# The dense part's products read their moving operand in turns from two runs of 256 words

## The chip, the cores and the metric

The kernel runs on one core of a Trainium2 chip. The metric is the device time of one execution in microseconds (us). A core has a matrix engine (TensorE, PE in the profile, with its weight loads as PEld), VectorE (DVE), ScalarE (ACT), GpSimd (POOL), and a queue engine (SyncE, SP) that issues transfers here. A product on TensorE holds a stationary operand of up to 128 columns and streams a moving operand of up to 512 columns through it; the result goes to PSUM.

## The reference

Three stages: attention with two fixed masks, a mixture of experts with soft slots, and a dense two-layer network. The change lies in the last one, and its inputs are:

```python
def _moe_ref(x, phi, w1, w2):          # 2304 tokens, 512 wide; 8 experts with 4 slots each
    logits = x @ phi
    ...                                # slot_out: 32 rows of 512, one for each slot
    c = softmax(logits, axis=1)        # 2304 x 32
    return c @ slot_out

def _moe2_ref(x, w_in, w_out):         # w_in 512 x 2048, w_out 2048 x 512
    h = x @ w_in
    g = np.where(h > 0.0, h, np.exp(np.minimum(h, 0.0)) - 1.0)
    return g @ w_out                   # 2304 x 512
```

The weights w_in and w_out come as 64-bit floats and are decoded to 32 bits on the chip.

## The kernel before

Attention and experts take the first 126 us. After them the kernel never forms the experts' output x. Since x = c @ slot_out, the hidden layer is h = c @ (slot_out @ w_in), and the kernel forms M = slot_out @ w_in (tile `M4`, 2048 columns) in two-part numbers that fill 128 rows.

The moving operand of the hidden layer is `cT`: the routing weights c, transposed, one column for each of the 2304 tokens. It is copied from `c4` by `emit_ct` (line 1026), sixteen copies of 32x576 elements: for each of four batches four row groups, in turn on ScalarE, GpSimd and, for two of them, VectorE. These copies are written between the last experts' products.

The dense part is a list of units. A unit (`unit_nodes`, line 1256) is one block of 128 hidden columns (f, 16 of them) for one group of tokens (`groups`: four groups of 512 tokens and one of 256). It consists of:

- one product at line 1264, stationary 128 columns of `M4`, moving 512 (or 256) columns of `cT`;
- exponential and ReLU on ScalarE (lines 1268, 1271), the combination on VectorE (line 1274), which together give g;
- the split of g in a high part on ScalarE (line 1280, f_hi) and a low part on VectorE (line 1284, f_lo). [...]
- for each of the 4 (or 2) token tiles of 128 three products with w_out at lines 1312 to 1314: high by high, high by low, low by high. Here the moving operand is a row block of w_out, 512 columns, itself split in two parts (lines 1213 and 1216).

The very last token tile of the last unit has its three products in two halves of 256 columns. [...] Units are counted from 0. All products of the dense part, 79 units of them and unit 0, accumulate in PSUM, six banks for the outputs and two for the hidden layer. An output tile whose run of f blocks ends is evicted to `part` (lines 1347, 1349) or, at last, added up in `ob` and stored (lines 1353 and 1360).

Beside that the weights are decoded, four steps a block: line 991 on ScalarE, lines 995, 999 and 1005 on VectorE. Lines 991 and 999 read every second 32-bit word of the 64-bit numbers. M's further columns are formed at lines 1153 to 1180.

The order of all this work on the engines is set by `list_order` (line 87), a list scheduler that runs when the program is built. It gets nodes with an engine, an estimated duration, what they depend on and a key (when they are due), and takes them by key. The due times step on by the estimated product times: `now += groups[gi][1] / 512 * ((3.6 if u < FULL else 2.72) + 0.2267)` (line 1121), where 2.72 is four token tiles of 0.68, and 0.68 and 0.2267 are also the durations of the nodes of lines 1317 and 1292. Before the dense part has filled up, warm-up products (line 1373, bfloat16, 256 columns) fill waits of TensorE. Loads on SyncE's queue stand in the same list.

Of the kernel before, what the change touches and what calls it, by code (L numbers as in the profile page):

```python
# [9 lines left out]
F32R = mybir.dt.float32r  # L10
I32 = mybir.dt.int32
BF16 = mybir.dt.bfloat16
AF = mybir.ActivationFunctionType
# [6 lines left out]
def attn_moe_mlp(ctx, tc, q, k, v_l, v_s, phi, w1, w2, w_in, w_out, out):  # L20
    nc = tc.nc
    B, S, D = 4, q.shape[2] // 4, 64
    NT, DM = out.shape
# [46 lines left out]
    FULL = 1  # L70
    FT, FW, M0 = 7.5, 0.9, ((0, 128), (128, 128), (256, 256))
# [184 lines left out]
    with tc.manual_schedule():  # L256
# [765 lines left out]
        cT = pers[:, 0:NT].rearrange("p (b s) -> p b s", b=B).bitcast(F32R)  # L1022
        M4 = pers[:, NT:NT + DFF].bitcast(F32R)
        e0r = e0.bitcast(F32R)

        def emit_ct(eng, a, b):
            o, i = cT[32 * a:32 * a + 32, b], c4[32 * b:32 * b + 32, a // 2].bitcast(F32R)
            if eng == "A":
                nc.scalar.activation(out=o, in_=i, func=AF.Copy)
            else:  # L1030
                (nc.vector if eng == "V" else nc.gpsimd).tensor_copy(out=o, in_=i)
# [54 lines left out]
        cTf = cT.rearrange("p b s -> p (b s)")  # L1086
        NF = DFF // 128
        groups = [(t, min(512, NT - t)) for t in range(0, NT, 512)]
# [167 lines left out]
        def unit_nodes(u):  # L1256
# [35 lines left out]
            x = link("h", node("P", 0.2267 * z, [m_done[f]], T - 4.1 - SL, f_h, ("h", rel_h)))  # L1292
# [9 lines left out]
            for s in range(n // 128):  # L1302
                def f_o(s=s):
                    if f == f0:
                        ops[si, gi, s] = ps_out.tile([128, DM], F32, tag="o", name="ops")
                    o, c = ops[si, gi, s], slice(128 * s, 128 * s + 128)
                    if full:
                        nc.tensor.matmul(o, t["g"][:, c], dec_of["o", f // 4, f % 4], start=(f == f0), stop=False)
                        return
                    hi, lo = w_tile(wo_hi, 0, f).bitcast(F32R), w_tile(wo_lo, 5, f).bitcast(F32R)  # L1310
                    for x in halves(u, s):
                        nc.tensor.matmul(o[:, x], t["hi"][:, c], hi[:, x], start=(f == f0), stop=False)  # L1312
                        nc.tensor.matmul(o[:, x], t["hi"][:, c], lo[:, x], start=False, stop=False)  # L1313
                        nc.tensor.matmul(o[:, x], t["lo"][:, c], hi[:, x], start=False, stop=(f == f1 - 1 and x.stop == 512))  # L1314

                rel_o = []
                y = link("o", node("P", 0.9 if full else 0.68, [x, d3[1, f // 4, f % 4, 0] if full else w_done[f]],
                                   T + 0.68 * s, f_o, ("o", rel_o) if f == f0 else None))
# [6 lines left out]
                if f == f0:  # L1325
                    o_rel.append(rel_o)
                    o_due.append(T + 0.68 * s)
                    part_n[si, gi, s] = len(o_rel) - 1
                if f == f1 - 1:
                    ev_n.append((si, gi, s, f0, f1, y, T + 0.68 * s, halves(u, s)))  # L1330
# [51 lines left out]
def _lay(np, q, k, v, moe_phi, **rest):  # L1382
# [17 lines left out]
    return dict(rest, q=lay(q), k=lay(k), v_l=vl, v_s=vs, moe_phi=phi, moe_w1=w1, moe_w2=w2)  # L1400
# [25 lines left out]
```

## Time and profile before

| | us |
|---|---|
| median of 3 timed runs | 358.36 (358.03 to 359.21) |
| the profiled execution, its time | 357.83 |
| its span, first to last instruction | 356.1 |
| TensorE busy | 336.8 |
| VectorE busy | 260.8 |
| ScalarE busy | 248.7 |
| GpSimd busy | 57.4 |

Times in the profile count from the first instruction of the span. [...] Each execution has a time outside the span (1.7 us in the profiled one).

### The profile page before, as it was taken

To read this page: it belongs to the slowest core of one execution; us is meant where nothing else is said; L and a number is where in the kernel's file an instruction comes from. 1 tells how busy PE (TensorE), PEld (TensorE's weight loads), DVE (VectorE), ACT (ScalarE), POOL (GpSimd) and SP (SyncE) were. 2 spreads that over 40 slices of the span, in tenths; PEclk is the share of its full clock that TensorE was granted. 3 is DMA by queue.
4 is the path that set the end of the run, shared out by engine and by line. 5 is a ranking of instruction groups with operands and counts; after the bars stand their busy time and mean duration, and the time that the engine had idled before them with its cause. 6 is when DMAs were issued, how large, how long until landed. Compare 5 with 4: busy or idle time off the path is not lost.

```text
span 356.1 us, 6955 instructions
## 1 busy us (share of the span) xinstructions
PE 336.8 (95%) x2678; PEld 249.6 (70%) x2678; DVE 260.8 (73%) x574; ACT 248.7 (70%) x488; POOL 57.4 (16%) x106
## 2 busy tenths in 40 slices
PE   5589899998999999999999999999999999999995
PEld 4378777773333257787888788888878888888884
DVE  6999889743706069999999999997755674576741
ACT  9588999982216079999977877767656666666650
POOL 8888534520214000000000000000000000000000
PEclk9999999999999999999999999999999999999999
DMA  7999999999999998750006041000000030032301
GB/s 280 401 418 411 424 421 421 424 407 420 430 424 417 404 403 323 250 221 0 3 0 238 0 162 74 2 0 0 2 0 1 2 119 0 31 118 88 118 2 59
DMA packets 15328, 70.50 MB, mean 198 GB/s; under 512 B 1600, under 2 KB 2112, under 8 KB 12352
## 3 DMA queue, kind: packets, MB, share of 16 engines
q1 hardware_dynamic: 15296, 70.06, 49.3%
q8 instruction: 21, 0.34, 0.4%
q14 instruction: 11, 0.09, 0.1%
HBM read 65.34 MB, written 4.72 MB: 197 GB/s over the span
## 4 chain that ended last, share of the span: by engine, by line
PE 74%; DVE 8%; DMA 6%; ACT 4%; POOL 4%; issue 2%; DVEq 0%; SPq 0%; POOLq 0%
PE ops L1312 18%; PE ops L1314 18%; PE ops L1313 18%; DMA q<-in_moe_w_dram 6%; PE hps L1264 5%; PE s_ps L923 3%; ACT bd L657 2%; DVE sc L589 2%; PE o_ps L670 2%; PE mps L1153 1%; ACT xw L696 1%; PE xtps L786 1%; DVE sm L613 1%; POOL bd L659 1%; DVE ss L604 1%
## 5 line engine op out<-in xcount | busy, mean ns | idle before, releaser
L1274 DVE SCALAR_TENSOR_TENSOR g<-hps,g 128x512 f32<-128x512 f32 (+1 forms) x80 | 50.7, 634 | 17.8 <-ACT g L1271 17.3
L1268 ACT ACTIVATE g<-hps 128x512 f32<-128x512 f32 (+1 forms) x80 | 44.8, 560 | 13.6 <-PE hps L1264 12.2
L1271 ACT ACTIVATE g<-g 128x512 f32<-128x512 f32 (+1 forms) x80 | 47.5, 594 | 1.5
L1280 ACT ACTIVATE ghi<-g 128x512 fp32r<-128x512 f32 (+1 forms) x40 | 23.7, 591 | 18.3 <-DVE g L1274 16.5
L1314 PE MATMUL ops<-w,glo 128*128 128x512 f32 (+1 forms) x93 | 36.0, 387 | 0.0
L1280 ACT ACTIVATE rings<-g 128x512 fp32r<-128x512 f32 (+1 forms) x39 | 23.6, 606 | 17.3 <-DVE g L1274 16.5
L1312 PE MATMUL ops<-wh,rings 128*128 128x512 f32 x80 | 31.6, 396 | 0.0
L1312 PE MATMUL ops<-w,ghi 128*128 128x512 f32 (+1 forms) x81 | 31.4, 388 | 0.0
L1313 PE MATMUL ops<-w,ghi 128*128 128x512 f32 (+1 forms) x81 | 31.4, 387 | 0.0
L1313 PE MATMUL ops<-wl,rings 128*128 128x512 f32 x80 | 31.2, 390 | 0.0
L1314 PE MATMUL ops<-wh,glo 128*128 128x512 f32 x80 | 31.2, 390 | 0.0
L1264 PE MATMUL hps<-pers 128*128 128x512 f32 (+1 forms) x80 | 30.3, 380 | 0.0
L657 ACT ACTIVATE bd<-tr 32x288 f32<-32x288 f32 (+1 forms) x60 | 28.7, 479 | 1.3
L1313 PE MATMUL ops<-w,rings 128*128 128x512 f32 x64 | 25.0, 391 | 0.0
L1312 PE MATMUL ops<-w,rings 128*128 128x512 f32 x64 | 25.0, 391 | 0.0
L1314 PE MATMUL ops<-wh,rings 128*128 128x512 f32 x62 | 24.3, 392 | 0.0
L1312 PE MATMUL ops<-wh,ghi 128*128 128x512 f32 x62 | 24.2, 391 | 0.0
L1313 PE MATMUL ops<-wl,ghi 128*128 128x512 f32 x62 | 24.2, 391 | 0.0
L1314 PE MATMUL ops<-w,rings 128*128 128x512 f32 x52 | 20.2, 389 | 0.0
L1284 DVE TENSOR_TENSOR glo<-g,ghi 128x512 fp32r<-128x512 f32 (+1 forms) x24 | 15.2, 633 | 6.8 <-ACT ghi L1280 4.5
L1314 PEld LDWEIGHTS ops<-w,glo 128*128 128x128 f32 x93 | 17.5, 188 | 3.6
L670 PE MATMUL o_ps<-bd,v 128*64 128x128 f32 x288 | 18.1, 276 | 1.2 <-ACT bd L657 0.9
(230 smaller groups left out, 757.8 us busy)
## 6 DMA issues: line engine op xcount, KB each, us to landing
v<-in_moe_w_dram SPq DMA_DIRECT2D x3, 2048.0 KB, 11.8
w<-in_moe_w_in_dram SPq DMA_DIRECT2D x3, 2048.0 KB, 8.0
out_dram<-ob SPq DMA_DIRECT2D x17, 256.0 KB, 2.0
w<-in_moe_w_dram SPq DMA_DIRECT2D x2, 2048.0 KB, 11.6
xw<-in_moe_w_dram SPq DMA_DIRECT2D x4, 1024.0 KB, 11.9
xw<-in_moe_w_out_dram SPq DMA_DIRECT2D x2, 2048.0 KB, 7.8
q<-in_q_dram SPq DMA_DIRECT2D x6, 576.0 KB, 8.0
kB<-in_k_dram SPq DMA_DIRECT2D x8, 288.0 KB, 7.5
```

The lines of the kernel that those rows point to most:

```text
L657: nc.scalar.activation(out=o, in_=i, func=AF.Copy)
L670: nc.tensor.matmul(o[64 * e:64 * e + 64, j, :], v_t[p][:, max(i - 1 + k, 0), e, :], pt[:, 4 * j + 2 * e + k], start=(k == 0), stop=(k == 1),)
L923: nc.tensor.matmul(hp[32 * g:32 * g + 32, :], siT[:, POS[c], :], w_at(2 * a + g // 2, 0, 2 * c + g % 2), start=(c == CO[0]), stop=(c == CO ...
L1264: nc.tensor.matmul(t["ps"], M4[:, 128 * f:128 * f + 128], cTf[:, t0:t0 + n], start=True, stop=True)
L1268: nc.scalar.activation(out=t["g"], in_=t["ps"], func=AF.Exp)
L1271: nc.scalar.activation(out=t["g"], in_=t["g"], func=AF.Relu, scale=-1.0, bias=1.0)
L1274: nc.vector.scalar_tensor_tensor(out=t["g"], in0=t["ps"], scalar=0.0, in1=t["g"], op0=ALU.max, op1=ALU.subtract)
L1280: nc.scalar.activation(out=t["hi"], in_=t["g"], func=AF.Copy)
L1284: nc.vector.tensor_tensor(out=t["lo"], in0=t["g"], in1=t["hi"].bitcast(F32), op=ALU.subtract)
L1312: nc.tensor.matmul(o[:, x], t["hi"][:, c], hi[:, x], start=(f == f0), stop=False)
L1313: nc.tensor.matmul(o[:, x], t["hi"][:, c], lo[:, x], start=False, stop=False)
L1314: nc.tensor.matmul(o[:, x], t["lo"][:, c], hi[:, x], start=False, stop=(f == f1 - 1 and x.stop == 512))
```

## The change

The products at lines 1264, 1308 and 1312 to 1314 get another access pattern for the moving operand, and for the output a pattern that is the same dense run in other words. `turns` takes a run of n words as two halves and reads them alternately: word 0 of the first, word 0 of the second, word 1 of the first, and so on. For the results to stand where they stood, the operand must be stored with its even elements in the first half and its odd elements in the second. For `cT` the copies do this, in pieces that end at the groups' bounds; for w_out the host does it with the columns. The stationary operands are as they were. The planner's numbers for a product go from 0.2267 to 0.216, and for a token tile from 0.68 to 0.648.

```diff
+    PO, PH = 0.648, 0.216
...
-        cT = pers[:, 0:NT].rearrange("p (b s) -> p b s", b=B).bitcast(F32R)
+        cTf = pers[:, 0:NT].bitcast(F32R)
...
+        def turns(v):
+            return v.rearrange("p (a x) -> p x a", a=2)
+
+        def pairs(v):
+            return v.rearrange("p (x a) -> p x a", a=2)
+
         def emit_ct(eng, a, b):
-            o, i = cT[32 * a:32 * a + 32, b], c4[32 * b:32 * b + 32, a // 2].bitcast(F32R)
...
+            for t0, n in groups:
+                u0, u1 = max(t0, S * b), min(t0 + n, S * b + S)
+                if u0 >= u1:
+                    continue
+                o = turns(cTf[32 * a:32 * a + 32, t0:t0 + n])[:, (u0 - t0) // 2:(u1 - t0) // 2]
+                i = pairs(c4[32 * b:32 * b + 32, a // 2, u0 - S * b:u1 - S * b].bitcast(F32R))
...
-            now += groups[gi][1] / 512 * ((3.6 if u < FULL else 2.72) + 0.2267)
+            now += groups[gi][1] / 512 * ((3.6 if u < FULL else 4 * PO) + PH)
...
-                nc.tensor.matmul(t["ps"], M4[:, 128 * f:128 * f + 128], cTf[:, t0:t0 + n], start=True, stop=True)
+                nc.tensor.matmul(
+                    pairs(t["ps"]), M4[:, 128 * f:128 * f + 128], turns(cTf[:, t0:t0 + n]), start=True, stop=True
+                )
...
-                        nc.tensor.matmul(o, t["g"][:, c], dec_of["o", f // 4, f % 4], start=(f == f0), stop=False)
+                        nc.tensor.matmul(
+                            pairs(o), t["g"][:, c], turns(dec_of["o", f // 4, f % 4]), start=(f == f0), stop=False
+                        )
...
-                    hi, lo = w_tile(wo_hi, 0, f).bitcast(F32R), w_tile(wo_lo, 5, f).bitcast(F32R)
+                    hi, lo = turns(w_tile(wo_hi, 0, f).bitcast(F32R)), turns(w_tile(wo_lo, 5, f).bitcast(F32R))
                     for x in halves(u, s):
-                        nc.tensor.matmul(o[:, x], t["hi"][:, c], hi[:, x], start=(f == f0), stop=False)
...
+                        y, q = pairs(o[:, x]), slice(x.start // 2, x.stop // 2)
+                        nc.tensor.matmul(y, t["hi"][:, c], hi[:, q], start=(f == f0), stop=False)
...
+    wo = rest["moe2_w_out"]
+    wo = wo.reshape(wo.shape[0], -1, 2).transpose(0, 2, 1).reshape(wo.shape)
```

The copies, on VectorE, stand between the last decoding ahead of the dense part and the transposition that forms the slots' matrix (`pers` holds `cT`, c is `c4`, xw the decoded weights). Before:

```order
L999 SCALAR_TENSOR_TENSOR xw<-kA,xw 128x256
L1005 SCALAR_TENSOR_TENSOR xw<-kA,xw 128x256
L1031 COPY pers<-c_1492 32x576 x2
L1076 STREAM_TRANSPOSE soT<-s_ps_96 128x128
L995 TENSOR_SCALAR xw<-xw 128x512
```

And after, where lines are those of the changed kernel:

```order
L1000 SCALAR_TENSOR_TENSOR xw<-kA,xw 128x256
L1006 SCALAR_TENSOR_TENSOR xw<-kA,xw 128x256
L1045 COPY pers<-c_1492 32x224x2
L1045 COPY pers<-c_1492 32x64x2
L1045 COPY pers<-c_1492 32x160x2
L1045 COPY pers<-c_1492 32x128x2
L1090 STREAM_TRANSPOSE soT<-s_ps_96 128x128
```

Two copies have become four, with pairs of words as their innermost step; on GpSimd eight have become sixteen and on ScalarE six twelve, at the same places.

In the dense part nearly the same products follow each other on TensorE. What the planner's new numbers move lies mostly on VectorE and ScalarE. One place is VectorE from the low part of unit 7 to that of unit 8 (the rows that write glo or rings are low parts, L1274 is the combination, L995, L999 and L1005 are decoding steps, wl is the low part of w_out). Before:

```order
L1284 TENSOR_TENSOR glo_1797<-g,ghi_1796 128x512
L1005 SCALAR_TENSOR_TENSOR xw<-xw 128x512
L995 TENSOR_SCALAR xw<-xw 128x512
L1274 SCALAR_TENSOR_TENSOR g<-hps,g 128x512
L999 SCALAR_TENSOR_TENSOR xw<-w_0_1_1743,xw 128x512
L995 TENSOR_SCALAR xw<-xw 128x512
L1284 TENSOR_TENSOR glo_1798<-g,rings 128x512
```

And after (1298 is the low part, 1288 the combination, 996, 1000 and 1006 the decoding, 1228 w_out's low part, 1192 a piece of M):

```order
L1298 TENSOR_TENSOR glo_1813<-g,ghi_1812 128x512
L1192 SCALAR_TENSOR_TENSOR pers<-mp,negm,mps 128x256
L996 TENSOR_SCALAR xw<-xw 128x512
L1006 SCALAR_TENSOR_TENSOR xw<-xw 128x512
L1000 SCALAR_TENSOR_TENSOR xw<-w_0_1_1759,xw 128x512
L1228 TENSOR_TENSOR wl_1809<-xw,wh_1808 128x512
L1006 SCALAR_TENSOR_TENSOR xw<-w_0_1_1759,xw 128x512
L996 TENSOR_SCALAR xw<-xw 128x512
L1288 SCALAR_TENSOR_TENSOR g<-hps,g 128x512
L1000 SCALAR_TENSOR_TENSOR xw<-w_0_1_1759,xw 128x512
L1228 TENSOR_TENSOR wl_1809<-xw,wh_1808 128x512
L1298 TENSOR_TENSOR glo_1814<-g,rings 128x512
```

Ten rows stand between the two low parts where five stood; the piece of M and the low parts of w_out came later or earlier by one unit.

## Rows read from the trace of the kernel before

**Rows 1.** The page's head: span, busy time of each engine; chain of work.

```profile
span 356.1 us, 6955 instructions
...
PE 336.8 (95%) x2678; PEld 249.6 (70%) x2678; DVE 260.8 (73%) x574; ACT 248.7 (70%) x488; POOL 57.4 (16%) x106
...
PE 74%; DVE 8%; DMA 6%; ACT 4%; POOL 4%; issue 2%; DVEq 0%; SPq 0%; POOLq 0%
PE ops L1312 18%; PE ops L1314 18%; PE ops L1313 18%; DMA q<-in_moe_w_dram 6%; PE hps L1264 5%; PE s_ps L923 3%; ACT bd L657 2%; DVE sc L589 2%; PE o_ps L670 2%; PE mps L1153 1%; ACT xw L696 1%; PE xtps L786 1%; DVE sm L613 1%; POOL bd L659 1%; DVE ss L604 1%
```

**Rows 2.** Stretches: bounds and length, busy us of engines, granted clock, DMA share, GB/s.

```profile
150.00:160.00 10.00, 10.00 (x46) 8.29 (x45) 9.88 (x18) 10.00 (x20) 0.00 (x0) 1.00 0.61 212
170.00:180.00 10.00, 10.00 (x45) 8.26 (x44) 10.00 (x18) 9.66 (x19) 0.00 (x0) 1.00 0.00 1
220.00:230.00 10.00, 10.00 (x45) 8.28 (x45) 10.00 (x19) 7.24 (x13) 0.00 (x0) 1.00 0.01 2
260.00:270.00 10.00, 10.00 (x45) 8.24 (x44) 5.41 (x8) 6.00 (x11) 0.00 (x0) 1.00 0.00 0
```

**Rows 3.** By line: ns min/median/max, first and last start; from the timeline: start, us.

```profile
L1264 PEld LDWEIGHTS hps<-pers x16: 187/188/188, 276.2 to 320.4; 128*128 128x128 f32 x16
L1264 PE MATMUL hps<-pers x16: 389/390/390, 276.4 to 320.6; 128*128 128x512 f32 x16
...
L1264 PEld LDWEIGHTS hps<-pers x6: 187/188/189, 336.0 to 342.8; 128*128 128x128 f32 x6
L1264 PE MATMUL hps<-pers x6: 277/278/278, 336.2 to 343.1; 128*128 128x256 f32 x6
...
L1308 PE MATMUL ops<-xw,g x4: 592/593/593, 131.9 to 133.2; 128*128 128x512 f32 x4
...
L1373 PE MATMUL wps<-ident x23: 272/273/283, 128.1 to 134.0; 128*128 128x256 bf16 x23
...
130.29 1.48 PE L1373 MATMUL wps<-ident 128*128 128x256 bf16 x12
...
131.93 1.88 PE L1308 MATMUL ops<-xw,g 128*128 128x512 f32 x4
```

**Rows 4.** The chain before the dense part (start, us, what) and TensorE's last product.

```profile
101.41 22.16 DMA q<-in_moe_w_dram
...
351.94 0.28 PE L1314 MATMUL ops<-w,glo 128*128 128x256 f32 x1
```

**Rows 5.** Timeline of the copies on three engines: start, us, idle time ahead.

```profile
105.37 5.59 POOL L1031 CAST pers<-c 32x576 fp32r<-32x576 f32 x8 [14.01 <-issue]
...
109.82 4.13 ACT L1029 ACTIVATE pers<-c 32x576 fp32r<-32x576 f32 x6
126.06 0.38 ACT L1065 ACTIVATE y<-o_ps 128x256 f32<-128x256 f32 x1 [12.11 <-PE o_ps L1012]
...
115.11 0.92 DVE L1031 CAST pers<-c 32x576 fp32r<-32x576 f32 x2
```

**Rows 6.** Timeline: low parts of units 8 and 14, and their first products.

```profile
152.11 0.69 DVE L1284 TENSOR_TENSOR glo<-g,rings 128x512 fp32r<-128x512 f32 x1
...
155.60 0.39 PE L1312 MATMUL ops<-wh,rings 128*128 128x512 f32 x1
...
173.24 0.68 DVE L1284 TENSOR_TENSOR glo<-g,ghi 128x512 fp32r<-128x512 f32 x1
...
175.02 0.39 PE L1312 MATMUL ops<-wh,ghi 128*128 128x512 f32 x1
```

**Rows 7.** Groups by line, 150 to 250 us: count, busy us, mean ns, idle ahead.

```profile
L1271 ACT ACTIVATE g<-g 128x512 f32<-128x512 f32 x34 | 22.0, 647 | 0.5
...
L991 ACT ACTIVATE xw<-w 128x512 f32<-128x512 f32 x15 | 10.4, 725 | 0.0
...
L991 ACT ACTIVATE xw<-xw 128x512 f32<-128x512 f32 x8 | 5.0, 685 | 1.4 <-DMA xw<-in_moe_w_out_dram 1.4
...
L999 DVE SCALAR_TENSOR_TENSOR xw<-w,xw 128x512 int32<-128x512 int32 x16 | 10.9, 684 | 0.0
```

More of the change, by code (lines that the diff above doesn't have):

```diff
@@ L1021, in attn_moe_mlp @@
         ND = dec.shape[1]
-        cT = pers[:, 0:NT].rearrange("p (b s) -> p b s", b=B).bitcast(F32R)
+        cTf = pers[:, 0:NT].bitcast(F32R)
         M4 = pers[:, NT:NT + DFF].bitcast(F32R)
         e0r = e0.bitcast(F32R)
-        def emit_ct(eng, a, b):
-            o, i = cT[32 * a:32 * a + 32, b], c4[32 * b:32 * b + 32, a // 2].bitcast(F32R)
[L1028 to L1031, printed above, removed]
+        groups = [(t, min(512, NT - t)) for t in range(0, NT, 512)]
+        def turns(v):
+            return v.rearrange("p (a x) -> p x a", a=2)
+        def pairs(v):
+            return v.rearrange("p (x a) -> p x a", a=2)
+        def emit_ct(eng, a, b):
+            for t0, n in groups:
[4 more added lines that the diff above has]
+                i = pairs(c4[32 * b:32 * b + 32, a // 2, u0 - S * b:u1 - S * b].bitcast(F32R))
+                if eng == "A":
+                    nc.scalar.activation(out=o, in_=i, func=AF.Copy)
+                else:
+                    (nc.vector if eng == "V" else nc.gpsimd).tensor_copy(out=o, in_=i)
         for e in range(NE - 1):
@@ L1084, in attn_moe_mlp @@
         ps_out = ctx.enter_context(tc.tile_pool(name="ps_out", bufs=6, space=PSUM))
-        cTf = cT.rearrange("p b s -> p (b s)")
         NF = DFF // 128
-        groups = [(t, min(512, NT - t)) for t in range(0, NT, 512)]
         dec_of = {("w", 0, c): dec[:, c] for c in range(4)}
@@ L1290, in link @@
                 return x
-            x = link("h", node("P", 0.2267 * z, [m_done[f]], T - 4.1 - SL, f_h, ("h", rel_h)))
+            x = link("h", node("P", PH * z, [m_done[f]], T - 4.1 - SL, f_h, ("h", rel_h)))
             x = link("e", node("A", 0.05 + 0.43 * z, [x], T - 3.7 - SL, f_e, ("g", rel_g)))
@@ L1307, in f_o @@
                     if full:
-                        nc.tensor.matmul(o, t["g"][:, c], dec_of["o", f // 4, f % 4], start=(f == f0), stop=False)
+                        nc.tensor.matmul(
+                            pairs(o), t["g"][:, c], turns(dec_of["o", f // 4, f % 4]), start=(f == f0), stop=False
+                        )
                         return
-                    hi, lo = w_tile(wo_hi, 0, f).bitcast(F32R), w_tile(wo_lo, 5, f).bitcast(F32R)
+                    hi, lo = turns(w_tile(wo_hi, 0, f).bitcast(F32R)), turns(w_tile(wo_lo, 5, f).bitcast(F32R))
                     for x in halves(u, s):
-                        nc.tensor.matmul(o[:, x], t["hi"][:, c], hi[:, x], start=(f == f0), stop=False)
-                        nc.tensor.matmul(o[:, x], t["hi"][:, c], lo[:, x], start=False, stop=False)
-                        nc.tensor.matmul(o[:, x], t["lo"][:, c], hi[:, x], start=False, stop=(f == f1 - 1 and x.stop == 512))
+                        y, q = pairs(o[:, x]), slice(x.start // 2, x.stop // 2)
+                        nc.tensor.matmul(y, t["hi"][:, c], hi[:, q], start=(f == f0), stop=False)
+                        nc.tensor.matmul(y, t["hi"][:, c], lo[:, q], start=False, stop=False)
+                        nc.tensor.matmul(y, t["lo"][:, c], hi[:, q], start=False, stop=(f == f1 - 1 and x.stop == 512))
                 rel_o = []
-                y = link("o", node("P", 0.9 if full else 0.68, [x, d3[1, f // 4, f % 4, 0] if full else w_done[f]],
-                                   T + 0.68 * s, f_o, ("o", rel_o) if f == f0 else None))
+                y = link("o", node("P", 0.9 if full else PO, [x, d3[1, f // 4, f % 4, 0] if full else w_done[f]],
+                                   T + PO * s, f_o, ("o", rel_o) if f == f0 else None))
                 if full:
@@ L1326, in unit_nodes @@
                     o_rel.append(rel_o)
-                    o_due.append(T + 0.68 * s)
+                    o_due.append(T + PO * s)
                     part_n[si, gi, s] = len(o_rel) - 1
                 if f == f1 - 1:
-                    ev_n.append((si, gi, s, f0, f1, y, T + 0.68 * s, halves(u, s)))
+                    ev_n.append((si, gi, s, f0, f1, y, T + PO * s, halves(u, s)))
         for u in range(len(work)):
```

2 lines of the change are left out of this document (1 added, 1 removed).

## The prediction

> **What bounds the kernel now.** I read the page's head and its chain of work first [rows 1]. TensorE is busy for 336.8 of 356.1 us, and of the chain that ended last 54% are the three products of lines 1312 to 1314 and 5% the product of line 1264. That is the dense part, from 134 us to 352 us. [...] A TensorE record overlaps the next one (0.39 us long, but started every 0.23 us), so a busy share of 1 is not yet a proof; the pitch is. In the steady stretch sixteen line-1264 products start between 276.4 and 320.6 us [rows 3], one for each unit of work, and a unit is thirteen products of 512 columns (one of line 1264, four times three). 44.2 us / 15 / 13 = 226.7 ns from start to start, with no gap anywhere in it. TensorE's own rate bounds 218 us of the 356.
>
> What sets 226.7 ns? [...] The weight load is not the bound: a 256-column product of the dense part has the same 188 ns load record as a 512-column one, and its length is smaller by 112 ns [rows 3], as the columns are halved.
>
> **The change part by part.** *The moving reads.* [...] No row shows the interleaved read itself, so I bound its pitch. [...] Above: the reads of every second word that other engines do here [rows 7]. ScalarE's line 991 reads with a step of two words and takes 685 to 725 ns where line 1271, which reads a dense row, takes 647 ns, 6% to 12% more. VectorE's line 999 takes 684 ns with such a read and line 1284 takes 0.68 to 0.69 us without [rows 6], no difference. 6% on top of 226.7 ns would be 240 ns.
>
> How many: 16 blocks of the hidden layer by 18 token tiles less the 2 tiles of the float32 unit are 286 groups of three. One of them is split in halves of 256. Line 1264 has 64 products of 512 and 16 of 256 columns. That makes 855 + 64 = 919 products of 512 columns, each 226.7 - 215.7 = 11.0 ns shorter: 10.1 us. The 22 of 256 columns give 5 ns each (278 against 273): 0.1 us. Sum of the gain on TensorE: **10.2 us**. [...]
>
> *The start* of the dense part does not move: it waits for the last expert weights, which land at 123.6 us after a transfer of 22 us on the chain [rows 4]. *The end* keeps its tail: from the last product at 351.94 us, eviction and stores to 356.1 us [rows 4].
>
> *The copies into the moving operand.* Sixteen copies of 32x576 become thirty-two shorter ones (POOL 8 to 16, ScalarE 6 to 12, VectorE 2 to 4), with a destination in two runs. Before, one takes 0.66 us on POOL, 0.68 on ScalarE, 0.45 on VectorE [rows 5]. If the second piece costs as much as a whole copy did, and it cannot well cost more than that, POOL ends 5.6 us later, at 116.6 us, ScalarE 4.1 us later, at 118.1 us, VectorE 0.9 us later, at 116.9 us. Each engine has nothing else until 126 us (ScalarE idles 12.1 us there), and the first reader is the product at 129.8 us. Cost on the path: nothing. Were that cover gone, it would be ScalarE's 4.1 us.
>
> *The host's order of w_out's columns* and the outputs: the products write PSUM in the old order, so evictions and stores are the same instructions. Decoding w_out reads the same bytes. Nothing.
>
> *The faster TensorE and what feeds it.* Each unit needs two VectorE and three ScalarE passes, and in the first 100 us of the dense part the weights' decoding runs beside them: VectorE is busy 9.88 to 10.00 of 10 us and ScalarE 10.00 at 150 us and 9.66 at 170 us [rows 2]. TensorE will want the same work in 95% of the time. What covers it is the lead: unit 8's last split ends at 152.80 us (152.11 + 0.69) and its first product starts at 155.60 us, 2.8 us later; the thinnest is unit 14 with 173.92 and 175.02 us, 1.1 us [rows 6]. The third product, the only one that reads that split, comes 0.45 us after the first. The planner's new numbers move decoding on VectorE: in the order of instructions, 48 instead of 45 rows now stand from the first weight split of the dense part up to unit 8's split. By start-to-start times of 0.60 us (0.34 for line 995) that is 1.8 us more work before it, while the product is due 0.8 us earlier: 2.8 - 1.8 - 0.8 leaves 0.2 us, or 0.6 for the third product. Up to unit 14's split 80 rows stand instead of 82, 1.2 us less work, against a product 1.7 us earlier: 0.6 us is left. So the cover is used up almost exactly. VectorE's own waits in that stretch were single ones of up to 0.6 us, and they may fall worse: between 0 and 2 us of TensorE stalls before 200 us. I take **0.5 us**. By 260 us VectorE is busy about half of the time [rows 2], and nothing is late.
>
> *Sum:* 10.2 - 0.5 = 9.7 us. The profiled execution took 357.83 us, 1.7 us more than its span; it becomes 348.1. It lies 0.5 us under the median of the three timed runs, 358.36, so against that: **348.7 us**.
>
> **The rivals.** *VectorE becomes the bound.* The rate comes, but the splits before 240 us are late again and again. Between 150 and 240 us TensorE would be done 4.3 us sooner; VectorE was busy throughout, and if it needed all of the time it took, those 4.3 us fall away: some 353 us. For it: the table of stretches. Against it: the leads of 3 us, which can be consumed, and the count of rows above.
>
> *The order of reading does not matter.* [...] Then only the order of instructions changed: 358.4 +- 1 us.
>
> *Slower: each word from another place costs.* By the code, TensorE reads dense pieces of 18 words or more everywhere before; now no two neighbouring reads touch. If the read port pays for a jump as ScalarE's does, 240 ns each, 930 products' worth of columns by 13.6 ns are 12.6 us: 371 us. [...]
>
> **How the numbers follow.** The rate comes and stalls stay under 2 us: 0.70, time 347.0 to 351. The rate comes and VectorE gives back 2 to 5.5 us: 0.10, up to 354. Rate unchanged: 0.09. Slower: 0.11. The last two are left out of the range, 347.0 to 354.0, whose lower end lies between the gain taken and that of the 213.3 ns bound. 0.3%, some 1.1 us, is about what a measurement of this kernel tells from no change: faster 0.80, same 0.09, slower 0.11.
>
> **What would show it.** The thirteen-product pitch at line 1264 in a quiet stretch: 2.80 us for a unit instead of 2.95 if the rate comes, 2.95 if order is nothing, 3.1 or more if jumps cost; the record of one product should shrink from 390 to about 379 ns. Gaps in TensorE between 145 and 200 us released by the splits, with leads near zero, would be VectorE's rival. Copies that end after 126 us would refute the cover. The start at 129.8 us and the 4 us tail should stand. The forecast is wrong if the pitch stays above 220 ns, or if the gaps sum to more than 2 us above those of before.

## The result and the profile after

| | before | after |
|---|---|---|
| median of the timed runs, us | 358.23 (358.03 to 359.21) | 354.33 (354.27 to 355.31) |
| the profiled execution, us | 357.83 | 354.27 |
| its span, us | 356.1 | 352.6 |

The ratio of the two medians is 0.989, with a 95% interval of 0.987 to 0.992. The change makes the kernel faster by 3.9 us. That is 0.3 us above the upper end of the range of 347.0 to 354.0, and 5.6 us above the forecast of 348.7.

In the changed kernel line 1264 has become 1276, the triple 1312 to 1314 has become 1329 to 1331, line 1274 is 1288, and the decoding lines 991, 995, 999 and 1005 are 992, 996, 1000 and 1006. The last of these reads every second word too: 992 and 1000 read the high words of the 64-bit numbers, 1006 the low ones.

The page's head and its chain of work, to be read against [rows 1]:

```profile
span 352.6 us, 7011 instructions
...
PE 332.7 (94%) x2679; PEld 251.4 (71%) x2679; DVE 268.7 (76%) x576; ACT 256.3 (73%) x494; POOL 63.1 (18%) x114
...
PE 55%; DVE 17%; ACT 15%; DMA 8%; issue 3%; POOL 2%; DVEq 0%; SPq 0%; POOLq 0%; ACTq 0%
```

TensorE's share of the chain has gone from 74% to 55%; VectorE's rose from 8% to 17%, ScalarE's from 4% to 15%. VectorE is busy 7.9 us longer and ScalarE 7.6 us longer. The copies, now in more pieces, account for 0.5 and 3.5 us of that; the rest comes from the dense part, which gives both engines the same instructions as before. That is the first sign of where the gain went.

**The rate came.** The hidden-layer product by line (shortest, median and longest in ns, then the first and last start) in the quiet stretch that [rows 3] shows of before; and from the timeline (start and length in us) the dense part's first product, two hidden-layer products in a row, and the last product:

```profile
L1276 PE MATMUL hps<-pers x17: 272/379/379, 276.0 to 320.9; 128*128 128x512 f32 x16, 128*128 128x256 f32 x1
```

```profile
130.10 0.65 PE L1276 MATMUL hps<-pers 128*128 128x256 f32 x2
...
276.02 0.38 PE L1276 MATMUL hps<-pers 128*128 128x512 f32 x1
...
278.82 0.38 PE L1276 MATMUL hps<-pers 128*128 128x512 f32 x1
...
348.32 0.28 PE L1331 MATMUL ops<-w,glo 128*128 128x256 f32 x1
```

A unit of thirteen products takes 278.82 - 276.02 = 2.80 us, so a product takes 215.4 ns where it took 226.7, and its record is 379 ns long instead of 390.

**Gaps came with it.** The stretches of [rows 2], and one over 140 to 260 us:

```profile
150.00:160.00 10.00, 9.84 (x46) 8.29 (x45) 10.00 (x18) 10.00 (x19) 0.00 (x0) 1.00 0.63 230
170.00:180.00 10.00, 10.00 (x48) 8.77 (x47) 9.97 (x17) 10.00 (x20) 0.00 (x0) 1.00 0.00 1
220.00:230.00 10.00, 10.00 (x48) 8.75 (x47) 9.59 (x16) 8.00 (x14) 0.00 (x0) 1.00 0.04 14
260.00:270.00 10.00, 10.00 (x46) 8.35 (x47) 6.31 (x10) 7.09 (x12) 0.00 (x0) 1.00 0.00 2
...
140.00:260.00 120.00, 116.96 (x539) 94.56 (x538) 117.66 (x198) 101.30 (x180) 0.00 (x0) 1.00 0.20 74
```

In those 120 us VectorE is now busy for 117.66 us and TensorE no longer for all of it. To size the gaps I took, over all TensorE products from the first of lines 1329 to 1331 to the last, each distance between starts that is more than 6% above the median pitch, and added up what lies above that pitch: 3.0 us before, 9.7 us after. The rate's 10.2 us less these 6.7 us make 3.5 us, and the profiled executions differ by 3.56 us. That the account closes so well is in part luck, since smaller terms that it leaves out cancel: outside the gaps the mean distance fell by 11.5 ns a product, not 11.0, but the first product starts 0.3 us later (130.10 us, 129.79 before) and unit 0's float32 products took 0.44 us longer.

**The float32 products got slower.** Unit 0's two products with w_out are in plain float32, at line 1308 before and at 1322 now, and show as four records; the change gave them the turns too. By line and from the timeline, against the 592 ns and the 1.88 us of [rows 3]:

```profile
L1322 PE MATMUL ops<-xw,g x4: 702/703/703, 132.2 to 133.8; 128*128 128x512 f32 x4
...
132.23 2.32 PE L1322 MATMUL ops<-xw,g 128*128 128x512 f32 x4
```

From start to start that is (2.32 - 0.70) / 3 = 540 ns where it was (1.88 - 0.59) / 3 = 429, so the four records together last 0.44 us longer. The same two-run turns that speed up the products of the split parts (type float32r, fp32r in the rows) from 226.7 to 215.4 ns slow the plain float32 ones.

**Whom TensorE waits for.** The largest of the weight loads' waits over the dense part after the change, and the same wait before, with the total, the times and the longest; then from the timeline after the change VectorE's work before such a wait ends, and the product that had waited:

```profile
PEld hps L1276 <- DVE g L1288: 5.8, 11, 1.0
...
PEld hps L1264 <- DVE g L1274: 1.5, 5, 0.5
```

```profile
189.19 1.67 DVE L1000 SCALAR_TENSOR_TENSOR xw<-w,xw 128x512 int32<-128x512 int32 x2
190.68 0.77 DVE L1298 TENSOR_TENSOR rings<-g,rings 128x512 fp32r<-128x512 f32 x1
191.28 1.64 DVE L1006 SCALAR_TENSOR_TENSOR xw<-w,xw 128x512 int32<-128x512 int32 x2
192.79 0.73 DVE L1288 SCALAR_TENSOR_TENSOR g<-hps,g 128x512 f32<-128x512 f32 x1
...
193.58 0.48 PE L1276 MATMUL hps<-pers 128*128 128x512 f32 x1 [0.57 <-DVE g L1288]
```

So 1.5 us in five pieces have become 5.8 us in eleven. The hidden-layer product needs one of two PSUM banks, and line 1288 frees it. At 192.79 us this line starts behind four decoding steps and a split, back to back without an idle moment. VectorE is late because of its work, not because it waits.

**What got longer.** The groups by line, 150 to 250 us, as in [rows 7]: count, busy us, mean ns:

```profile
L1285 ACT ACTIVATE g<-g 128x512 f32<-128x512 f32 x33 | 21.8, 662 | 0.3
...
L992 ACT ACTIVATE xw<-w 128x512 f32<-128x512 f32 x15 | 13.8, 925 | 0.0
...
L992 ACT ACTIVATE xw<-xw 128x512 f32<-128x512 f32 x8 | 7.8, 988 | 0.0
...
L1288 DVE SCALAR_TENSOR_TENSOR g<-hps,g 128x512 f32<-128x512 f32 x33 | 23.1, 700 | 0.4 <-ACT g L1285 0.3
L1006 DVE SCALAR_TENSOR_TENSOR xw<-w,xw 128x512 int32<-128x512 int32 x16 | 13.1, 826 | 0.0
L1000 DVE SCALAR_TENSOR_TENSOR xw<-w,xw 128x512 int32<-128x512 int32 x16 | 12.9, 824 | 0.0
```

Line 992 takes 925 and 988 ns where 991 took 725 and 685; line 1000 takes 824 ns and line 1006 826 ns where 999 and 1005 took 684. From start to start in a row of instructions (medians over the 26 blocks of the dense part) the step on ScalarE went from 0.56 to 0.77 us and the two on VectorE from 0.60 to 0.74 us; the shift of line 996, dense, stayed at 0.33 us. That makes 26 x 0.21 = 5.5 us more on ScalarE and 52 x 0.14 = 7.3 us more on VectorE. Only the three steps that read every second word are further apart. The other instructions' records are up to 7% longer (line 1285, which reads a dense row, 662 ns instead of 647), but from start to start they are as they were: 0.52 us for line 1285, 0.60 us for line 1288. Early in the trace the three steps were not slow yet: two of line 1000 that start before or among unit 0's products take 0.69 us each, one of line 1006 at 129.01 us takes 0.69 us, and two of line 992 in a row span 1.44 us, as two of line 991 did before.

```profile
128.28 0.69 DVE L1000 SCALAR_TENSOR_TENSOR xw<-xw 128x512 int32<-128x512 int32 x1
...
131.88 0.69 DVE L1000 SCALAR_TENSOR_TENSOR xw<-xw 128x512 int32<-128x512 int32 x1
```

**The copies** on the three engines, answering [rows 5]:

```profile
105.31 11.26 POOL L1045 CAST pers<-c 32x512 fp32r<-32x512 f32 x16 [14.01 <-issue]
...
109.76 7.62 ACT L1043 ACTIVATE pers<-c 32x512 fp32r<-32x512 f32 x12
126.37 0.38 ACT L1079 ACTIVATE y<-o_ps 128x256 f32<-128x256 f32 x1 [8.99 <-PE o_ps L1013]
...
116.69 1.37 DVE L1045 CAST pers<-c 32x448 fp32r<-32x448 f32 x4
```

They end at 116.6, 117.4 and 118.1 us. ScalarE still idles 9 us behind them, and the dense part starts at 130.1 us (129.8 before).

### The profile page after: what moved, and what is told of

The parts are those of the page before. It is cut to its first block, busy times and chain, and to the rows that moved or that the text cites. A ratio compares the mean times of both kernels' runs of the same rounds, so it can differ in the third digit from the quotient of the medians.

```text
span 352.6 us, 7011 instructions
## 1 busy us (share of the span) xinstructions
PE 332.7 (94%) x2679; PEld 251.4 (71%) x2679; DVE 268.7 (76%) x576; ACT 256.3 (73%) x494; POOL 63.1 (18%) x114
## 4 chain that ended last, share of the span: by engine, by line
PE 55%; DVE 17%; ACT 15%; DMA 8%; issue 3%; POOL 2%; DVEq 0%; SPq 0%; POOLq 0%; ACTq 0%
PE ops L1329 13%; PE ops L1331 13%; PE ops L1330 13%; DMA q<-in_moe_w_dram 6%; PE hps L1276 3%; PE s_ps L924 3%; ACT xw L992 2%; ACT bd L658 2%; ACT g L1285 2%; DVE sc L590 2%; ACT g L1282 2%; PE o_ps L671 2%; ACT part L1364 2%; DVE g L1288 2%; DVE xw L1006 2%
## 5 line engine op out<-in xcount | busy, mean ns | idle before, releaser
L1331 PE MATMUL ops<-w,glo 128*128 128x512 f32 (+1 forms) x93 | 35.0, 377 | 0.0
L1329 PE MATMUL ops<-wh,rings 128*128 128x512 f32 x80 | 31.1, 389 | 0.8 <-ACT part L1364 0.5
L1329 PE MATMUL ops<-w,ghi 128*128 128x512 f32 (+1 forms) x81 | 30.6, 378 | 0.0
L1330 PE MATMUL ops<-w,ghi 128*128 128x512 f32 (+1 forms) x81 | 30.5, 376 | 0.0
L1330 PE MATMUL ops<-wl,rings 128*128 128x512 f32 x80 | 30.3, 379 | 0.0
L1331 PE MATMUL ops<-wh,glo 128*128 128x512 f32 x80 | 30.3, 379 | 0.0
L1329 PE MATMUL ops<-w,rings 128*128 128x512 f32 x64 | 24.3, 379 | 0.0
L1330 PE MATMUL ops<-w,rings 128*128 128x512 f32 x64 | 24.3, 379 | 0.0
L1331 PE MATMUL ops<-wh,rings 128*128 128x512 f32 x62 | 23.6, 381 | 0.0
L1276 PEld LDWEIGHTS hps<-pers 128*128 128x128 f32 x80 | 15.1, 188 | 9.1 <-DVE g L1288 5.8
L1331 PE MATMUL ops<-w,rings 128*128 128x512 f32 x52 | 19.7, 379 | 0.0
```

The source lines that it names most:

```text
L1276: nc.tensor.matmul(pairs(t["ps"]), M4[:, 128 * f:128 * f + 128], turns(cTf[:, t0:t0 + n]), start=True, stop=True)
L1329: nc.tensor.matmul(y, t["hi"][:, c], hi[:, q], start=(f == f0), stop=False)
L1330: nc.tensor.matmul(y, t["hi"][:, c], lo[:, q], start=False, stop=False)
L1331: nc.tensor.matmul(y, t["lo"][:, c], hi[:, q], start=False, stop=(f == f1 - 1 and x.stop == 512))
```

## The experiments

The theory after the result, **collision**: TensorE's reads in turns slow those readers that take every second word, VectorE runs out of time, and TensorE waits for it. Its rivals: **order** (the planner's new numbers rearranged the work badly), and **rate** (a faster TensorE wants the same work in less time, and any reader suffers from its denser reads). All diffs are against the changed kernel. "Gaps" are those of TensorE as defined above, "steps" the start-to-start medians of lines 992, 1000 and 1006 over the dense part. Each ratio is to the kernel before as it was timed beside that run (medians from 357.97 to 358.23 us). In e6 VectorE mostly idles behind line 1000, so that its distance to the next start says nothing; its record has the usual 684 ns.

| run | us | ratio to before, 95% | pitch, ns | steps, us | gaps, us |
|---|---|---|---|---|---|
| before | 358.2 | | 226.7 | 0.56, 0.60, 0.60 | 3.0 |
| changed | 354.33 | 0.987 to 0.992 | 216 | 0.77, 0.74, 0.74 | 9.7 |
| e1, dense, new plan | 358.15 | 0.9995 to 1.002 | 227 | 0.56, 0.60, 0.60 | 3.4 |
| e2, decoding reads a dense run | 348.41 | 0.970 to 0.974 | 216 | 0.52, 0.60, 0.60 | 3.7 |
| e7, plan knows the slow steps | 353.90 | 0.987 to 0.990 | 216 | 0.77, 0.75, 0.75 | 8.2 |
| e8, old plan | 359.13 | 1.002 to 1.004 | 216 | 0.76, 0.74, 0.74 | 13.7 |
| e9b, low parts on GpSimd | 358.16 | 0.999 to 1.003 | 216 | 0.77, 0.75, 0.75 | 12.1 |
| e13, one step reads densely | 349.65 | 0.975 to 0.980 | 216 | 0.78, 0.61, 0.75 | 4.5 |
| e3, turns of 2 words | 454.73 | 1.267 to 1.270 | 333 | 0.57, 0.60, 0.61 | 1.9 |
| e4, turns of 16 words | 370.01 | 1.031 to 1.034 | 240 | 0.57, 0.60, 0.60 | 3.1 |
| e5, four runs | 410.94 | 1.145 to 1.149 | 283 | 0.57, 0.60, 0.60 | 2.4 |
| e6, sixteen runs | 551.76 | 1.538 to 1.543 | 435 | 0.61, -, 0.60 | 1.2 |
| e10, words 128 apart | 354.59 | 0.988 to 0.991 | 216 | 0.77, 0.74, 0.74 | 9.4 |
| e15, words 64 apart | 354.45 | 0.987 to 0.991 | 216 | 0.78, 0.74, 0.73 | 10.4 |
| e11, words 32 apart | 348.86 | 0.973 to 0.977 | 216 | 0.58, 0.60, 0.60 | 5.1 |
| e16, words 8 apart | 349.34 | 0.974 to 0.977 | 216 | 0.57, 0.60, 0.60 | 4.7 |
| e14, 32 apart, x too | 348.05 | 0.970 to 0.974 | 216 | 0.58, 0.60, 0.60 | 4.0 |

### Order, rate or collision

**e1** keeps the changed plan and the copies in pieces, but all reads are dense again:

```diff
         def turns(v):
-            return v.rearrange("p (a x) -> p x a", a=2)
+            return v.rearrange("p (x a) -> p x a", a=2)
...
-    wo = wo.reshape(wo.shape[0], -1, 2).transpose(0, 2, 1).reshape(wo.shape)
```

> The planner's numbers and the copies in pieces of the changed kernel, but every product reads its moving operand as one dense run again, and w_out's columns stay in order. Collision theory (TensorE's reads in turns slow the decoding steps that read every second word, lines 992, 1000 and 1006): products start every 226.7 ns, line 992 is back at 0.55 us from start to start and lines 1000 and 1006 at 0.60 us, and the time is within 1 us of the kernel before, 357.4 to 359.4 us. Order theory (the planner's new order is what makes TensorE wait): TensorE still waits 5 us or more before 260 us, and the time is above 361 us.

It takes 358.15 us and has the steps of before, in the very order in which the changed kernel has its instructions. The order alone costs nothing while TensorE reads densely, so it is not by itself what makes TensorE wait.

```profile
L992 ACT ACTIVATE xw<-w x16: 648/666/692, 148.2 to 204.9; 128x512 f32<-128x512 f32 x16
...
L1000 DVE SCALAR_TENSOR_TENSOR xw<-xw x10: 677/682/699, 144.9 to 240.5; 128x512 int32<-128x512 int32 x10
```

(Both from the view by line, 140 to 260 us: shortest, median and longest in ns, then the first and last start.)

**e2** leaves TensorE's turns as they are and makes the decoding read a dense run. It leaves out the choice of the right words, and its shift is a mask, so what it computes is not the network's output; instructions, shapes and order are those of the changed kernel:

```diff
+        def run(src):
+            return src.rearrange("p x a -> p (x a)")[:, 0:src.shape[1]]
...
-            nc.scalar.activation(out=dst, in_=src[:, :, 1].bitcast(F32), func=AF.Abs, scale=ESC)
+            nc.scalar.activation(out=dst, in_=run(src), func=AF.Abs, scale=ESC)
...
-                out=d, in0=src[:, :, 1], scalar=-0x80000000, in1=d, op0=ALU.bitwise_and, op1=ALU.bitwise_or
+                out=d, in0=run(src), scalar=-0x80000000, in1=d, op0=ALU.bitwise_and, op1=ALU.bitwise_or
...
-                out=d, in0=src[:, :, 0], scalar=29, in1=d, op0=ALU.logical_shift_right, op1=ALU.bitwise_or
+                out=d, in0=run(src), scalar=29, in1=d, op0=ALU.logical_shift_right, op1=ALU.bitwise_or
```

> The changed kernel, but the three decoding steps read as many words as a dense run instead of every second word (so the weights are decoded from the wrong words, and one shift became a mask; instructions, shapes and order are the same). Collision theory: lines 992, 1000 and 1006 take 0.52 to 0.60 us from start to start although products start every 216 ns, TensorE's waits before 260 us fall by 4 us or more, and the time is 348.5 to 350.5 us. Rate theory (products every 216 ns leave other engines fewer reads of any kind): these steps stay at 0.70 us or more and the time stays at 353.5 us or more. Order theory: 353.5 us or more too, with the steps at 0.60 us.

348.41 us, 0.3 us from the forecast. TensorE reads in turns every 216 ns, the dense readers beside it aren't slowed (0.52, 0.60 and 0.60 us), and the wait for line 1288 (1291 here) is back at 1.5 us:

```profile
L995 ACT ACTIVATE xw<-w x16: 621/634/686, 148.2 to 202.2; 128x512 f32<-128x512 int32 x16
...
L1003 DVE SCALAR_TENSOR_TENSOR xw<-xw x10: 676/680/682, 145.0 to 236.7; 128x512 int32<-128x512 int32 x10
```

```profile
PEld hps L1279 <- DVE g L1291: 1.5, 3, 0.8
```

So rate falls too. The loss needs both sides: TensorE in turns, and another engine in steps of two.

### How much lies in the plan

**e7** tells the planner what the steps take now; **e8** gives the changed kernel the old estimates of the products:

```diff
-            n = node("A", 0.05 + 0.47 * z, deps, key - 3.0, f_abs, None if h0 else ("dec", rel), at)
+            n = node("A", 0.05 + 0.70 * z, deps, key - 3.0, f_abs, None if h0 else ("dec", rel), at)
...
-            n = node("V", 0.07 + 0.53 * z, [n], key - 1.4, step(dec_2))
-            n = node("V", 0.07 + 0.53 * z, [n], key - 0.7, step(dec_3))
+            n = node("V", 0.07 + 0.67 * z, [n], key - 1.4, step(dec_2))
+            n = node("V", 0.07 + 0.67 * z, [n], key - 0.7, step(dec_3))
```

```diff
-    PO, PH = 0.648, 0.216
+    PO, PH = 0.68, 0.2267
```

> The changed kernel; only the planner's estimates of the three slowed decoding steps are raised to what the trace of the changed kernel shows (0.75 us for 512 words on ScalarE, 0.74 us on VectorE). The steps stay slow. If TensorE's 6 us of new waits come from the order that the planner chose with wrong times, they fall by 2 us or more, to 349.5 to 352 us. If VectorE simply has too much work before 250 us, the time stays within 1 us of 354.3 us.

> The changed kernel with the planner's old numbers for a product (0.2267 and 0.68 us), so its order is that of the kernel before. Products every 216 ns and slowed decoding steps as in the changed kernel. If the amount of work on VectorE before 250 us decides, 353.3 to 355.3 us, the same as the changed kernel. If the moved rows (48 instead of 45 before unit 8's low part) cost as the prediction counted, 0.5 to 2 us less: 352.3 to 353.8 us.

e7 ends at 353.90 us, which the intervals don't tell from the changed kernel. Its gaps are 1.5 us smaller, but its first product starts 0.8 us later, at 130.91 us: knowing the lengths doesn't give VectorE the time that it lacks. e8 ends at 359.13 us, slower than before and outside both of its expectations. So the new order is the better one, and the order theory falls. With the old due times the whole gain of the rate is lost, so the two planner numbers of the change are worth 4.8 us here, where e1 shows them worth nothing under dense reads. Whether that takes the slowed steps, or a product every 216 ns is enough, no run shows: the old due times were not combined with steps of normal length.

### Taking work off VectorE

**e9b** moves the low parts of w_out to GpSimd, which is idle in the dense part (the planner's numbers are e7's):

```diff
             def f_lo():
-                nc.vector.tensor_tensor(
+                nc.gpsimd.tensor_tensor(
...
-            x = node("V", 0.6, [x] + ([d3[1, 1, c, 0] for c in range(4)] if f == 8 else []), key + 0.7, f_lo)
+            x = node("G", 1.2, [x] + ([d3[1, 1, c, 0] for c in range(4)] if f == 8 else []), key + 0.1, f_lo)
```

> The changed kernel with the planner told the slower decoding (0.70 and 0.67), and with the low parts of w_out (16 subtractions of 0.6 us) moved from VectorE to GpSimd, which is idle in the dense part. If VectorE's time is what TensorE waits for, and GpSimd's reads disturb nobody: VectorE gets back some 16 x 0.69 = 11 us, TensorE's waits fall from 8 us to about 4, about 350 us. If GpSimd's subtraction holds VectorE up (or takes so long that w_out comes late): 354 us or more.

358.16 us, 4.3 us worse than e7; the gaps go from 8.2 to 12.1 us. GpSimd's subtraction takes 1.3 to 3.1 us, and VectorE's integer steps have single instances of 1.5 and 1.9 us beside it:

```profile
L1228 POOL TENSOR_TENSOR w<-xw,w x8: 1275/1592/3127, 201.5 to 249.1; 128x512 fp32r<-128x512 f32 x8
...
L996 DVE TENSOR_SCALAR xw<-xw x26: 392/418/1504, 143.4 to 243.8; 128x512 int32<-128x512 int32 x26
...
L1000 DVE SCALAR_TENSOR_TENSOR xw<-xw x10: 689/826/1908, 145.0 to 245.4; 128x512 int32<-128x512 int32 x10
```

Work given to GpSimd came back as longer instructions on VectorE: the eight of line 1000 that overlap a subtraction on GpSimd take 1.28 us in the median, the others 0.83 us, and splits of line 1298 beside one take up to 1.74 us.

**e13** takes away one of the three step-two reads. ScalarE writes the signed value into a tile of its own (`sg`), and the shift and the sign step read that:

```diff
+            if tmp is not None:
+                nc.scalar.activation(out=tmp, in_=src[:, :, 1].bitcast(F32), func=AF.Copy, scale=ESC)
+                return
...
-                out=d, in0=src[:, :, 1], scalar=-0x80000000, in1=d, op0=ALU.bitwise_and, op1=ALU.bitwise_or
+                out=d, in0=src[:, :, 1] if tmp is None else tmp.bitcast(I32), scalar=-0x80000000, in1=d, op0=ALU.bitwise_and, op1=ALU.bitwise_or
```

> The changed kernel with one of the three reads of every second word taken away: ScalarE writes the scaled high word with its sign into a tile of its own, and the shift (line 996) and the sign (line 1000) read that tile densely; ScalarE's read and the last step's stay. One such tile only, so ScalarE's next piece waits for the sign of this one. Theory 'step-two reads are slowed one by one': the sign step falls from 0.74 to 0.60 us or below, the other two stay at 0.77 and 0.74, VectorE gets back 26 x 0.14 = 3.6 us, TensorE's waits fall by 1 to 3 us, 351 to 353 us; 354 or more if the wait for the one tile takes it back. Theory 'VectorE as a whole is slowed by ScalarE's read': the sign step stays at 0.74.

349.65 us, over a microsecond better than its most hopeful figure. The sign step (line 1005 here) is back at normal length while the other two stay slow, one beside the other in the same trace:

```profile
L994 ACT ACTIVATE sg<-w x16: 861/884/947, 150.2 to 231.9; 128x512 f32<-128x512 f32 x16
...
L1005 DVE SCALAR_TENSOR_TENSOR xw<-sg,xw x26: 674/686/728, 145.0 to 258.0; 128x512 int32<-128x512 int32 x26
...
L1011 DVE SCALAR_TENSOR_TENSOR xw<-xw x10: 783/821/875, 146.3 to 259.9; 128x512 int32<-128x512 int32 x10
```

So the slowing belongs to the single instruction that reads in steps of two, not to VectorE as a whole; and TensorE's gaps fall from e7's 8.2 us (whose estimates for the two slow steps this kernel shares) to 4.5 us, when VectorE gets back 26 x 0.14 = 3.6 us: nearly one for one. The new tile also changes when the decoded blocks' buffers are taken, and the runs don't separate the two.

### Which turns are cheap

Four kernels change how TensorE takes its turns: **e3** two words from each run, **e4** sixteen, **e5** one word from each of four runs of 128, **e6** one from each of sixteen runs of 32. The planner's numbers stay.

```diff
-            return v.rearrange("p (a x) -> p x a", a=2)
+            return v.rearrange("p (a x w) -> p x a w", a=RUNS, w=TURN)
```

> The changed kernel with turns of two words: two words of the first run, two of the second. If the slow steps come from how often TensorE changes the run, they should cost about half as much more (0.65 us for lines 1000 and 1006 instead of 0.74), with products still every 216 ns: 351 to 353 us. If the gain of TensorE needs a change at every word, products go back towards 226.7 ns and the time towards 358 us. If only the pitch of 216 ns matters (rate theory), nothing changes: 354.3 us.

> The changed kernel with turns of sixteen words. [...]

> The changed kernel with turns of one word from four runs of 128 words (neighbouring reads 128 words apart instead of 256). If any change of run at every word has both effects, nothing changes: products every 216 ns, line 992 at 0.77 us and lines 1000 and 1006 at 0.74 us from start to start, 354.3 us. If the collision comes from two runs that lie 256 words apart, the decoding steps are back near 0.55 and 0.60 us and the time is 348.5 to 350 us. If a run must go on within two clocks to lose nothing, products get slower than 216 ns and the time rises above 355 us.

> [...]

All four are slower than dense reads: 333, 240, 283 and 435 ns a product. None of e3's figures had allowed for that. Two starts in a row of e3 and of e6:

```profile
300.50 0.50 PE L1332 MATMUL ops<-w,glo 128*128 128x512 f32 x1
300.83 0.50 PE L1330 MATMUL ops<-w,ghi 128*128 128x512 f32 x1
```

```profile
400.44 0.63 PE L1330 MATMUL ops<-w,ghi 128*128 128x512 f32 x1
400.87 0.63 PE L1331 MATMUL ops<-w,ghi 128*128 128x512 f32 x1
```

One word from each of two runs is not a point on a smooth scale; of these patterns it alone is faster than dense. And in all four the steps are at their normal length: of all the patterns tried only those in which TensorE takes 512 columns in 216 ns slow the step-two readers; in e3 and e4 the runs are as far apart, and nothing is slowed (0.57 us, and 0.60 to 0.61 us).

### Is it the distance

**e10, e15, e11 and e16** keep two runs and one word a turn, but let the runs stand side by side in blocks: runs of 128, 64, 32 and 8 words, so that the two words of a turn are that far apart. The products with x are dense in these four. **e14** has runs of 32 for all products. The form, for 32:

```diff
+        HALF_ = 32
+
         def turns(v):
-            return v.rearrange("p (a x) -> p x a", a=2)
+            return v.rearrange("p (k a x) -> p k x a", a=2, x=HALF_)
...
-    wo = wo.reshape(wo.shape[0], -1, 2).transpose(0, 2, 1).reshape(wo.shape)
+    wo = wo.reshape(wo.shape[0], -1, 32, 2).transpose(0, 1, 3, 2).reshape(wo.shape)
```

> The products with w_out take their two words from runs of 128 that stand side by side in blocks of 256, so the two words are 128 words apart, not 256; the products with x (one in thirteen) read densely again. Theory 'saturated reads': whatever pattern lets TensorE take 512 columns in 216 ns leaves the readers of every second word less room, so the pitch stays 216 ns, the three decoding steps stay at 0.74 to 0.77 us and the time is about 355 us (354.3 of the changed kernel and some 70 dense products at 11 ns more). Theory 'distance': the slowing hangs on the 256 words between the two words, so the steps fall to 0.56 and 0.60 us and the time to about 349 us. Theory 'the gain hangs on the 256 words': pitch of 227 ns or above, time 358 us or more.

> w_out in turns from two runs of 64 words in blocks of 128, x densely: the distance is 64. Runs of 128 gave slow steps (0.77/0.74) and 354.6 us, runs of 32 normal steps (0.575/0.60) and 348.9 us. 'Distance': it falls on one side or the other, with 349 us or 354.5 us; steps between (0.65/0.67) and 351 to 352 us would speak for something that counts the passes from block to block, of which this has four, runs of 32 eight, runs of 128 two.

> The same with runs of 32 words in blocks of 64: the two words are 32 words apart, and TensorE passes on to the next block eight times in a product. 'Saturated reads': pitch 216 ns, steps 0.74 to 0.77 us, about 355 us. 'Distance': pitch 216 ns, steps 0.56 and 0.60 us, about 349 us. If passing from block to block costs as a jump does (16 words a turn gave 240 ns for 32 jumps), 8 jumps would give about 220 to 225 ns and 357 us or more.

> The same with runs of 8 words in blocks of 16: distance 8, 32 passes from block to block in a product. If a pass costs as the jumps of 16-word turns did (240 ns for 32 of them), the pitch is 227 to 240 ns, and 358 to 370 us. If a pass costs nothing (8 of them cost nothing), 216 ns, steps at 0.57/0.60 us and 349 us. If two words that stand 8 apart can't be read like two that stand 32 apart, the pitch is that of dense reads, 227 ns, and about 358 us.

> Turns from two runs of 32 words in blocks of 64 for all products of the dense part, those with x too. If the distance decides, the pitch is 216 ns throughout, the steps stay at 0.57 and 0.60 us, and the 70 dense products of the run before give back some 11 ns each, 0.7 us: about 348.2 us, the fastest of all. If the copies of x in blocks come late, 349 or more.

The pitch is 216 ns in all five. The steps fall on two sides. View by line, 140 to 260 us, of e15 (64 apart) and then of e11 (32 apart):

```profile
L992 ACT ACTIVATE xw<-w x16: 646/892/1071, 148.4 to 207.5; 128x512 f32<-128x512 f32 x16
...
L1000 DVE SCALAR_TENSOR_TENSOR xw<-xw x10: 753/828/879, 145.3 to 244.5; 128x512 int32<-128x512 int32 x10
```

```profile
L992 ACT ACTIVATE xw<-w x16: 676/719/785, 148.1 to 202.8; 128x512 f32<-128x512 f32 x16
...
L1000 DVE SCALAR_TENSOR_TENSOR xw<-xw x10: 670/687/694, 144.8 to 237.2; 128x512 int32<-128x512 int32 x10
```

At 256, 128 and 64 words the steps are equally slow and the time is 354.3 to 354.6 us; at 32 and 8 they are normal and the time is 348.9 to 349.3 us. So 216 ns a product is not enough to slow them, and 'saturated reads' falls. There is nothing between the two levels, though the number of blocks a product passes goes from 1 to 2, 4, 8 and 32: an effect that grows with the passes would have shown as steps in between. Passing to the next block costs nothing that shows in the pitch, not even with 32 blocks.

e14 takes the turns of 32 to the products with x as well: 348.05 us (347.92 to 348.72), a ratio of 0.972 to before (0.970 to 0.974), the lowest median of all. It lies 0.8 us under e11's, where 0.7 us was expected of the products with x, but the single times of the two overlap (e11: 348.39 to 349.83). Its head and chain:

```profile
span 346.3 us, 7011 instructions
...
PE 70%; ACT 9%; DVE 8%; DMA 8%; POOL 3%; issue 2%; DVEq 0%; SPq 0%; POOLq 0%; ACTq 0%
```

What stays open is why distances of 64, 128 and 256 words disturb a reader in steps of two (0.73 to 0.74 us on VectorE) while 32 and 8 do not (0.60 us). Distance, run length and block size changed together, so the runs don't say which of them it is. Storing the high and the low words of the weights in runs of their own was not tried.

## Why the prediction missed

**The rate term came out right, its argument is not shown.** No run shows where the 215.7 ns that the sum takes for a product, or the 213.3 ns at the range's lower end, would come from; in their place the runs showed 215.4 ns in the quiet stretch, a record of 256 columns went from 278 to 272 ns where the sum took 273, and e2, in which the gaps are only 0.7 us above those of before, ends 0.3 us from the forecast. Nor do they show that two runs are faster because each of them goes forward more slowly: with four runs and with sixteen, each of which goes forward more slowly still, a product takes 283 and 435 ns. The float32 records, put in turns, went from 429 to 540 ns, a cost of 0.44 us that the sum put at nothing. So that the number came out was partly luck; why two runs are faster stays open.

**Start, copies and tail came close.** The dense part's first product starts at 130.10 us instead of 129.79. The copies were bounded at 116.6, 118.1 and 116.9 us and ended at 116.6, 117.4 and 118.1, VectorE's 1.2 us later than its bound but far ahead of the reader at 130.1 us. The tail from the last product to the end is 352.6 - 348.3 = 4.3 us (4.2 before).

**The step that failed** is the term of 0.5 us for TensorE's stalls; it measured 6.7 us. It failed in its durations. I worked the leads out with "start-to-start times of 0.60 us (0.34 for line 995)", taken from the trace of before, and counted rows. Three of the four decoding steps changed their length: 0.21 us on ScalarE and twice 0.14 us on VectorE, 26 times each. I had weighed the step-two reads of lines 991 and 999 only as a price list for TensorE's own read, never as work that TensorE's new read could slow. With lengths as they were before, as in e2, the gaps grow by 0.7 us, close to the 0.5 taken, and in e14, which decodes the real words, by 1.0 us: counting rows was good enough.

**The place was wrong as well.** I watched the splits' leads: 0.2 to 0.6 us was to be left of them. They held, with 1.3 us at unit 8 and 1.75 us at unit 14 (against 2.8 and 1.1 before, [rows 6]):

```profile
154.56 0.69 DVE L1298 TENSOR_TENSOR glo<-g,rings 128x512 fp32r<-128x512 f32 x1
...
156.55 0.38 PE L1329 MATMUL ops<-wh,rings 128*128 128x512 f32 x1
...
173.80 0.67 DVE L1298 TENSOR_TENSOR glo<-g,ghi 128x512 fp32r<-128x512 f32 x1
...
176.22 0.38 PE L1329 MATMUL ops<-wh,ghi 128*128 128x512 f32 x1
```

What ran late was line 1288, which frees the PSUM bank of the next hidden-layer product. That wait stood in the trace of before with 1.5 us, and I did not price it.

**The rivals.** VectorE as the bound had 0.10 and came true in its effect, 354.3 us against "some 353", with 6.7 us given back where the chances allowed 2 to 5.5. Its mechanism was another: not that TensorE's shorter time left VectorE too little (e2 refutes that), but that VectorE's own work grew. That the order of reading does not matter fell with 215.4 ns. The rival that each word from another place costs fell for two runs of the float32r products, with 215.4 ns, and held for the patterns with four and sixteen runs, with 283 and 435 ns.

**The range** ended at 354.0 because VectorE's rival was sized by what TensorE would gain between 150 and 240 us, 4.3 us, with up to 5.5 us allowed. Nothing in that sizing allowed for VectorE's own work to grow.

## What to carry to other kernels

When one engine's reads get a new pattern, the durations of every engine that works beside it are part of the change, as the steps of 0.60 us that took 0.74 us were here: take the durations from a run with the new pattern before trusting an account of leads. Where an engine's busy time rises though its instructions are the same, look for the group whose mean changed and ask what pattern it reads. A float32r product that streams one word in turns from two runs 32 or 8 words apart took 216 instead of 227 ns here and left VectorE's steps at 0.60 us; e14 is the form to use for such products. A plain float32 product should not get it: here its records took 540 instead of 429 ns, in e14 too, and a kernel that leaves that one product dense was not run.

## What was not expected of the hardware

- A dense run of 512 float32r words takes 226.7 ns, one word in turns from two runs 216 ns, two words in turns 333, sixteen words 240, four runs 283, sixteen runs 435 ns; passing through 32 blocks in a product shows no cost.
- A plain float32 record of 512 words goes the other way: 429 ns from start to start with dense reads, 540 ns in turns of one word from two runs.
- While TensorE reads in turns at 216 ns from runs 64, 128 or 256 words apart, reads of every second word get longer: on ScalarE from 0.56 to 0.77 or 0.78 us for 512 words, on VectorE from 0.60 to 0.73 or 0.74 us. Dense reads stay as far apart as they were (0.52 us for line 1285, 0.60 us for line 1288), though their records are up to 7% longer. With runs 32 or 8 words apart VectorE's reads stay at 0.60 us and ScalarE's are at 0.58 and 0.57 us.
- Beside GpSimd subtractions single integer steps of VectorE (lines 996 and 1000 in e9b) take 1.5 and 1.9 us instead of 0.42 and 0.83 us.
